# Holding the left keys and values of a memory-augmented recurrence by slot, with fewer and wider left matmuls

## The chip, the cores and the metric

The kernel runs on one core of one Trainium2 chip. The metric is the device time of one execution in microseconds; lower is better. Before the change the median of three runs is 1785.58 us (1778.69 to 1788.85).

## What is computed

The result is the sum of the input, an attention with memory, and a dense GELU block, all on 2048 tokens of width 1024 in bf16. The dense block reads all tokens at once. The attention is a recurrence: 64 segments of 32 tokens one after the other, where each segment sees 8 memory rows, and the first 8 rows of its own output are the memory of the next one.

```python
mem = mem0                                  # [8, 1024]
for s in range(64):
    xs = xn[:, 32 * s:32 * s + 32, :]
    h = concatenate([mem, xs], axis=1)      # 40 rows
    q, k, v = h @ Wq, h @ Wk, h @ Wv        # 32 heads of 128
    scores = where(mask, q @ k.T * scale, -1e9)   # memory rows see by the causal order of 40
    o = softmax(scores) @ v @ Wo
    mem = o[:, :8, :]
    outs.append(o[:, 8:, :])
out = x + concatenate(outs) + (gelu(xn @ w1 + b1) @ w2 + b2)
```

## The kernel before, in words

**Two stages.** The first (until about 410 us) makes the layer norm and the dense block, and turns the normalized rows into per-segment tiles in DRAM. The second is the recurrence; the change is in it alone, but for a few loads at the border.

**Weights.** A segment needs Wq, Wk, Wv and Wo whole, 64 tiles of 512 KB ("units", written as a letter, a block of rows and a half of the heads). 47 of them stay in SBUF. 17 a segment are streamed through a ring of six buffers (`RING`, `start_stream`, L273 to L285): when PE is done with one streamed unit, its buffer goes to the next in the order of use. Two of the 17 don't come from DRAM: they are kept in PSUM banks, and VectorE copies them into the buffer (`copy_bits`, L273), each as two halves of 128x512 uint32. The strings of `PLACED`, one for each of the four places of a segment in its group (`i4 = s % 4`), say at which unit of each pass of eight a streamed unit stands.

**Passes.** A segment goes through K, Q, K, Q, V, V (two halves of 16 heads; eight units each, `half_pass`, matmuls at L830) and then 16 output units (L1089). A unit of a pass is four matmuls that use four column groups of the array at once, with 512 columns each. PE's order is the order in which the code is written; the functions handed to a pass in `at` are issued after the unit with that number. `scores` (L947, L953), `sums` (L985, L991) and `values` (L1039, L1045) of one half of the heads are put between units of later passes in that way.

**Main and left rows.** The stationary operand of a projection holds 32 rows. For a segment these "main" rows are 24 of its tokens and the 8 memory rows. The remaining 8 tokens of each segment are "left" rows: those of four segments are put together in a second stationary tile (`hrL`), and one "left pass" of eight units makes their keys, queries or values for four segments. Each group of four segments has six left passes. In the old kernel they stand at i4 = 3 (K of half 0, V of half 1), 0 (K of half 1, V of half 0), 1 and 2 (Q). So a part of the left rows belongs to the next group while the present one isn't finished: `keep_q` saves queries in PSUM, and `moved_values` (L1191) holds the left values of half 1 in a tile of their own until they may be written. The first six resident units of the next left pass are issued at the end of the segment before ("lead", `lead_products`), where PE would wait for the memory rows.

**Attention of left rows.** In `scores`, each of 16 heads has one matmul of its main keys with 40 query columns (L947) and one of its left keys (32 rows of four segments) with 16 columns (L953). Four heads run at once in the four column groups. As left keys of all four segments are met, a mask by segment (`mask_left`, L977) takes out three quarters of the left probabilities. In `values`, four column blocks c each have a pair of matmuls of 64 rows with the main values (L1039, 80 columns) and a pair with the left values (L1045, 32 columns).

**Around it.** The key rows come out of PSUM by ScalarE (L882), and VectorE transposes them in blocks of 32 (L896); queries take L909 and L913 in two halves (`turn_q`). `q_left` (L925) puts the left queries of this segment into the first eight columns. `put_mem` (L320, L330) turns the 8 memory rows into the next segment's tile; L1243 adds the dense block's part to the result, which is loaded from DRAM (`hr_home<-res_d`). At i4 = 1, and in the last segment, the output pass also makes the 32 left rows, with four column tiles of 512 columns instead of two (`left_o`). Loads other than weights are issued by ScalarE in the first seven segments and by GpSimd after that; weights go through SP's queue.

## Time and profile before

| | |
|---|---|
| median of three runs | 1785.58 us |
| the profiled execution | 1788.29 us |
| its span, first to last instruction | 1786.6 us |
| granted TensorE clock | 0.998 |
| ScalarE work | 670.5 us |
| GpSimd work | 300.4 us |
| HBM read and written | 573.43 MB and 28.90 MB |

The profile is one execution. Each row of a group has a line of the kernel, an engine, an operation with what it writes and reads, the number of instructions, then the busy time with the mean of one in ns, and the idle time of the engine ahead of it with what ended that. Rows of the timeline have the start in us from the span's start, the time that a piece took, and the instructions merged in it. PE's durations hold some 0.17 us of latency for each matmul; matmuls overlap, so that intervals between starts tell what one costs. "issue" stands for idle time that nothing in the profile explains.

### The profile page before, as it was taken

Reading aid. Unit: us, or ns where it says so; the run is one execution under the profiler, and the core shown is the slowest. Engines: PE = TensorE matmul, PEld = TensorE weight load, DVE = VectorE, ACT = ScalarE, POOL = GpSimd, SP = SyncE. Lnnn points to the kernel's source line nnn. Section 1 sums busy time; section 2 is a strip of 40 time slices with the busy share of each in tenths; the row PEclk is TensorE's granted clock in tenths of the full one; section 3 lists DMA queues with packets and bytes.
Section 4 is the critical chain, followed back from the end, with each engine's and each line's share of the span. In section 5 each row is a group of like instructions: output and inputs, shape, how many; then the busy total and the mean of one; then the engine's idle time right before and its main releaser. Section 6 shows DMA issues by size and latency. Waiting matters only on the chain.

```text
span 1786.6 us, 70503 instructions
## 1 busy us (share of the span) xinstructions
PE 1697.1 (95%) x30600; PEld 867.5 (49%) x30600; DVE 987.9 (55%) x2642; ACT 670.5 (38%) x1709; POOL 300.4 (17%) x586
## 2 busy tenths in 40 slices
PE   9999999998999999999999999999999999999988
PEld 5444444444445544444545444454445445445444
DVE  7657483825555555555555555555555555555544
ACT  6334251603333333333333333343334333333333
POOL 0000002401231111111121211111121111111111
PEclk9999999999999999999999999999999999999999
DMA  9455312779999999999999999999999999999998
GB/s 278 146 167 169 91 45 71 267 277 335 387 390 388 387 374 383 380 383 367 393 378 382 374 381 393 389 388 389 375 387 400 389 389 394 380 378 396 378 376 316
DMA packets 232827, 594.37 MB, mean 333 GB/s; under 512 B 57715, under 2 KB 88035, under 8 KB 232516
## 3 DMA queue, kind: packets, MB, share of 16 engines
q1 hardware_dynamic: 197584, 567.08, 84.3%
q0 software_dynamic: 16896, 16.85, 2.8%
q10 hardware_dynamic: 18036, 5.94, 1.3%
q8 instruction: 239, 3.92, 0.9%
q14 instruction: 72, 0.59, 0.1%
HBM read 573.43 MB, written 28.90 MB: 337 GB/s over the span
## 4 chain that ended last, share of the span: by engine, by line
PE 70%; DMA 18%; DVE 4%; issue 3%; ACT 3%; ACTq 1%; SPq 1%; DVEq 0%
PE acc L830 36%; PE acc L1089 11%; PE ps L534 10%; DMA u<-Wc_O 10%; PE ps L662 6%; DMA u<-Wc_V 5%; PE ps L693 3%; PE acc L1039 1%; ACTq L459 1%; ACT mixed L999 1%; PE mixed L947 1%; SPq L521 1%; DMA hr_home<-res_d 1%; DVE pd_main L1012 1%; PE mixed L320 1%
## 5 line engine op out<-in xcount | busy, mean ns | idle before, releaser
L830 PE MATMUL acc<-u,hr_home 128*32 128x512 bf16 x11520 | 763.6, 380 | 19.7 <-DMA u<-Wc_V 10.2
L830 PEld LDWEIGHTS <-hr_home 128*32 128x32 bf16 x12288 | 337.8, 96 | 303.2 <-issue 45.2
L830 PE MATMUL acc<-u,hrL 128*32 128x512 bf16 x2880 | 253.0, 382 | 4.0 <-DMA hrL<-rowsL_d 2.1
L534 PE MATMUL ps<-u 128*128 128x512 bf16 (+1 forms) x992 | 195.1, 358 | 0.4 <-DMA u<-in_B_w_dram 0.4
L273 DVE TENSOR_SCALAR u<-kept 128x512 uint32<-128x512 uint32 x254 | 163.1, 684 | 48.0 <-PE acc L830 40.6
L1089 PE MATMUL acc<-u,d_oL 128*32 128x512 bf16 x2592 | 170.4, 380 | 13.0 <-issue 10.2
L882 ACT CAST d_oL<-acc 128x512 bf16<-128x512 f32 x143 | 82.0, 584 | 253.9 <-PE acc L830 220.9
L662 PE MATMUL ps<-u 128*128 128x512 bf16 x672 | 146.0, 379 | 0.0
L534 PEld LDWEIGHTS <-u 128*128 128x128 bf16 x992 | 91.6, 98 | 102.1 <-DMA u<-in_B_w_dram 0.6
L1089 PE MATMUL acc<-u,kq 128*32 128x512 bf16 (+1 forms) x2696 | 132.4, 320 | 8.1 <-DMA u<-Wc_O 6.4
L1012 DVE TENSOR_TENSOR pd_main<-kq,mixed 128x320 bf16<-128x320 bf16 x128 | 62.5, 488 | 129.2 <-ACT mixed L999 129.2
L909 ACT CAST kq<-acc 128x256 bf16<-128x256 f32 x256 | 89.4, 375 | 109.7 <-PE acc L830 76.6
L1089 PEld LDWEIGHTS <-kq 128*32 128x32 bf16 x3344 | 87.4, 96 | 84.0 <-ACT kq L1058 24.2
L1276 POOL DMA_DIRECT2D out_dram<-hr_home x168 | 85.4, 516 | 220.5 <-DVE hr_home L1243 220.5
L913 DVE STREAM_TRANSPOSE kq<-kq 128x256 bf16<-128x256 bf16 x256 | 98.2, 422 | 42.8 <-ACT kq L909 42.7
L886 ACT CAST kq<-acc 128x512 bf16<-128x512 f32 x128 | 75.2, 588 | 114.1 <-PE mixed L953 111.7
L977 DVE TENSOR_TENSOR kq<-kq,mixed 128x96 bf16<-128x96 bf16 (+1 forms) x256 | 38.1, 190 | 143.8 <-ACT kq L967 87.2
L830 PEld LDWEIGHTS <-hrL 128*32 128x32 bf16 x3072 | 86.3, 96 | 58.4 <-issue 3.7
L662 PEld LDWEIGHTS <-u 128*128 128x128 bf16 x672 | 65.5, 98 | 78.8 <-DVE u L619 0.4
L611 ACT ACTIVATE u<-ps,b1col 128x512 bf16<-128x512 f32 x112 | 76.5, 684 | 64.5 <-PE ps L534 61.7
L1089 PEld LDWEIGHTS <-d_oL 128*32 128x32 bf16 x2592 | 64.0, 96 | 69.5 <-issue 23.5
L999 ACT ACTIVATE mixed<-mixed,small_consts 128x160 f32<-128x160 f32 x256 | 94.2, 368 | 8.4
(127 smaller groups left out, 1910.5 us busy)
## 6 DMA issues: line engine op xcount, KB each, us to landing
u<-Wc_K SPq DMA_DIRECT2D x256, 512.0 KB
u<-Wc_V SPq DMA_DIRECT2D x256, 512.0 KB
u<-Wc_O SPq DMA_DIRECT2D x256, 512.0 KB
u<-Wc_Q SPq DMA_DIRECT2D x192, 512.0 KB
u<-in_B_w_dram SPq DMA_DIRECT2D x28, 512.0 KB
u<-in_A_Wq_dram SPq DMA_DIRECT2D x13, 512.0 KB
u<-in_A_Wv_dram SPq DMA_DIRECT2D x12, 512.0 KB
u<-in_A_Wk_dram SPq DMA_DIRECT2D x9, 512.0 KB
```

Of the source, the lines that this page charges most:

```text
L273: nc.vector.tensor_single_scalar(out=out, in_=in_, scalar=0, op=ALU.bitwise_or)
L534: nc.tensor.matmul(ps[:, SEG * s0:SEG * s1].rearrange("p (s t) -> p s t", t=SEG), lhsT=w1_sb[fb // 2][:, kt, (fb % 2) * P:(fb % 2 + 1) * P ...
L611: nc.scalar.activation(out=xb[:, :], in_=ps[:, :], func=ACT.Identity, bias=b1col[:, fb:fb + 1], scale=1.0)
L662: nc.tensor.matmul(ps[:, :], lhsT=gts[fc // 4][:, fc % 4, t * P:(t + 1) * P], rhs=w2_sb[fc // 2][:, fc % 2, cs], start=(fc == 0), stop=(fc ...
L830: nc.tensor.matmul(o, lhsT=lhs[:, i, :], rhs=m, start=(i == seq[0]), stop=(i == seq[-1]), tile_position=(0, 32 * j),)
L882: cp(out=out, in_=ps.rearrange("p (h e) -> p h e", e=32))
L909: nc.scalar.copy(out=q_home[:, h0:h1, NL:40], in_=ps[:, 32 * h0:32 * h1].rearrange("p (h e) -> p h e", e=32))
L913: nc.vector.transpose(out=half, in_=half)
L999: nc.scalar.activation(out=mixed[:, 160 * b:160 * b + 160], in_=mixed[:, 0:160], func=ACT.Exp, scale=-1.0, bias=off[:, b:b + 1],)
L1012: nc.vector.tensor_tensor(out=pdA.rearrange("p c b q -> p b c q"), in0=prA[:, None, :, :].to_broadcast([P, 2, 4, 40]), in1=dd, op=ALU.mult,)
L1089: nc.tensor.matmul(acc[r0:r0 + rows, 0:256 * len(blocks)], lhsT=lhsT, skip_group_check=True, rhs=o_columns(t, k, blocks), start=start, sto ...
L1276: loads.dma_start(out=out_flat[rows, 256 * j:256 * j + 256], in_=res[32 * j:32 * j + NX, :])
```

## The change

Left rows of a group are put in the order (token, segment) instead of (segment, token), so that the column `[..., i4]` of every fourth element is the 8 rows of one segment ("slot"). With that:

- `scores` takes the left keys of only this segment: 8 rows of four heads make one stationary tile of 32 columns, and one matmul meets it with the 16 left query columns of all four heads, 64 columns. The mask takes out the products of unlike heads.
- left values are laid out by slot too (`by_slot`, two transposes on VectorE), so that `values` has one pair of left matmuls with 128 columns for all four blocks.
- the left rows are renewed slot by slot (`renew_left`, copies on GpSimd, on VectorE in the first seven segments) in one tile that both groups share. Left passes stand at i4 = 0 (K, K), 1 (V of half 0), 2 (Q of half 0, V of half 1), 3 (Q of half 1); the double output pass stands at i4 = 3. Queries and values are made in the last group as well.
- the left accumulators are taken out of PSUM as soon as their last product is issued (`left_done`), ahead of the main ones of the same pass; `turn_qL` copies on ScalarE.
- `keep_q`, `moved_values` and the special cases of the last segment go. The strings of `PLACED` and some places change.

The core of the diff:

```diff
-SCORES_0 = (6, 6, 6, 5)
+SCORES_0 = (6, 6, 6, 6)
-ATTEND = (0, 0, 0, 1)
-VALUES_0 = ((4, 4), (4, 4), (4, 4), (3, 5))
-SUMS_1 = (6, 7, 6, 5)
+ATTEND = (0, 0, 1, 0)
+VALUES_0 = ((4, 4), (4, 4), (3, 5), (4, 4))
+SUMS_1 = (6, 6, 5, 7)
...
-    "..SS...." ".S..S..." "S....S.." "....S..S" "....S..." "S..S...S" "...S..S." "S....S.S",
-    "...SS..." ".S..S..." "..S..S.." "....SS.." ".S......" "S..S...S" "...S..S." "S....S.S",
-    ".SS....." "S...S..." "S....S.." "....S..S" "....S..." "S..S...S" "...S..S." "S....S.S",
-    "..SS...." ".S..S..." "S.....S." "....S..S" "....S..." "...SS..S" "...S..S." "S....S.S",
+    "..SS...." ".S..S..." "S....S.." "S......S" "S......." "S.S.S..." "...S.S.." "S....S.S",
+    ".SS....." "S...S..." ".S.S...." "....S..S" "....S..." "S..S.S.." "...S..S." "S....SS.",
+    "..SS...." ".S..S..." "S.....S." "....S..S" "..S....." "...SS..S" "...S..S." "S....SS.",
+    "...SS..." ".S..S..." "..S..S.." "....SS.." ".S......" "S..S...S" "...S..S." "S....SS.",
...
+    def renew_left(rows, s0, s1, eng):
+
+        eng.tensor_copy(
+            out=hL.rearrange("p k (t s) -> p k t s", s=GRP)[:, :, :, s0:s1],
+            in_=rows.rearrange("p (k s t) -> p k t s", k=KT, s=GRP)[:, :, :, s0:s1],
+        )
...
-            left_k = [first or (i4 == 3 and more), i4 == 0]
-            left_q = [first or (i4 == 1 and more), first or (i4 == 2 and more)]
-            left_v = [i4 == 0, first or (i4 == 3 and more)]
-            left_o = i4 == 1 or final
+            left_k = [i4 == 0] * 2
+            left_q = [first or i4 == 2, first or i4 == 3]
+            left_v = [first or i4 == 1, first or i4 == 2]
+            left_o = i4 == 3
...
+                    if left and left_done and i == order[-1]:
+                        left_done(psL)
...
+            def by_slot(u, t):
+
+                nc.vector.transpose(out=t, in_=t)
+                nc.vector.transpose(
+                    out=VL[u].rearrange("p (s n) -> p s n", s=GRP), in_=t.rearrange("p (n s) -> p s n", s=GRP)
+                )
...
-                turn(ps, qL[u][:, :, :], nc.vector.tensor_copy)
+                turn(ps, qL[u][:, :, :], nc.vector.tensor_copy if first else nc.scalar.copy)
...
+                keys = ko_flat[u].rearrange("p (j n s) -> p j n s", j=4, s=GRP)
...
-                    for j in range(4):
-                        q = slice(32 * j, 32 * j + 32)
-                        nc.tensor.matmul(
-                            sB[q, c, :].rearrange("p (a b) -> p a b", b=NL), lhsT=kL[u][:, 4 * j + c, :],
-                            rhs=qL_ends[:, 4 * j + c, :, :],
...
+                for j in range(4):
+                    q = slice(32 * j, 32 * j + 32)
+                    nc.tensor.matmul(
+                        sB[q, :, :, :], lhsT=keys[:, j, :, i4], rhs=qL_ends[:, 4 * j:4 * j + 4, :, :],
...
+                place = qL_slots[0] if first or VALUES_0[i4][0] < VALUES_0[i4][1] else ko_slots[0]
+                pdB = q_all[:, 512:640] if u else place[:, :, i4]
...
-                    for r in rs:
-                        q = slice(64 * r, 64 * r + 64)
-                        nc.tensor.matmul(
-                            oV[r].rearrange("p c b (e q) -> p c b e q", q=NL)[:, c, :, ::4, :],
-                            lhsT=VL[u][q, c * P:(c + 1) * P], rhs=pdB[q, c, :, :, :],
...
+                for r in rs:
+                    q = slice(64 * r, 64 * r + 64)
+                    nc.tensor.matmul(
+                        av[r][:, 0:320].rearrange("p (n e q) -> p n e q", n=8, q=NL)[:, :, ::4, :],
+                        lhsT=VL[u][q, i4 * P:(i4 + 1) * P], rhs=pdB[q, :].rearrange("p (n a q) -> p n a q", n=8, q=NL),
...
-            psK, psKL = half_pass("K", 0, left_k[0], {})
+            psK, psKL = half_pass(
+                "K", 0, left_k[0], {0: [lambda: by_slot(i4 - 2, qL_flat[i4 - 2])]} if i4 >= 2 else {},
+                lambda ps: turn_kL(ps, 0),
+            )
...
+            def first_queries(ps):
+
+                turn_qL(ps, 0)
                 q_left(0)
+
+            psQ, psQL = half_pass("Q", 0, left_q[0], {} if left_q[0] else {1: [lambda: q_left(0)]}, first_queries)
             turn_q(psQ)
-            if left_q[0] and not first:
-                turn_qL(psQL, 0)
...
+            psQ1, psQ1L = half_pass("Q", 1, left_q[1], at, lambda ps: turn_qL(ps, 1))
+            if left_q[1]:
                 q_left(1)
             turn_q(psQ1)
-            if left_q[1] and not first:
-                turn_qL(psQ1L, 1)
```

More of the change, by code (lines that the diff above doesn't have):

```diff
@@ L511, in turn_R @@
                     pairs = [(res_d[seg + 1, :, :].rearrange("(j t) c -> t j c", j=4), rows)]
[L512 to L518 removed]
+                pairs += [(both[w][slot:SEG:GRP, :, :], halves[w][NX:SEG, :, :]) for w in range(2)]
                 for o, r in pairs:
@@ L797, in unit_done @@
                         small.popleft()()
-        hT, hL = nxt["hT"], nxt["hL"]
-        kL, VL = [None] * 2, [None] * 2
+        hT = nxt["hT"]
+        VL = [late.tile([P, 512], BF16, name=f"VL{u}") for u in range(2)]
         led = {}
@@ L870, in half_pass @@
                     if left and i not in ahead:
-                        product(w, i, t, hL, psL, order)
+                        product(w, i, t, hL, psL, order, True)
                     if first and (w, i, u) == IN_PSUM:
@@ L902, in turn_kL @@
             def turn_kL(ps, u):
-                kL[u] = left_keys[u]
-                turn(ps, kL[u], nc.vector.tensor_copy if first else nc.scalar.copy)
+                turn(ps, ko[u], nc.vector.tensor_copy if first else nc.scalar.copy)
             def turn_q(ps):
@@ L1175 @@
             st["V", 1] = values_out(psV1, v_home, nc.scalar.copy)
-            apart = left_v[1] and not first
-            if apart:
-                ahead_v = left_keys[1]
-                rows_out(psV1L, ahead_v, nc.scalar.copy)
+            if left_v[1]:
+                staged(1)(psV1L)
             if first:
-                left_values(1, psV1L)
+                by_slot(1, hr_home)
+                renew_left(left_rows_in, 0, 2, mover)
+                load_x_rows(s + 1, loads)
             loads.dma_start(out=homes[s % 2], in_=res_d[s + 1, :, :])
-            if first:
-                load_left_rows(g + 1, loads)
-            def moved_values():
-                VL[1] = late.tile([P, 512], BF16, name="VL1")
-                (nc.vector if s < EARLY_SEGS else nc.gpsimd).tensor_copy(out=VL[1].rearrange("p (h t) -> p h t", t=SEG), in_=ahead_v)
+            if i4 == 3 and g + 2 < NGRP:
+                load_left_rows(g + 2, left_rows_in[:, :], loads)
             at = {VALUES_1[i4]: [lambda: values(1, (0, 1))]}
-            if apart:
-                at[VALUES_1[i4] + 1] = [moved_values]
             psX = new_acc()
```

201 lines of the change are left out of this document (74 added, 127 removed).

## The prediction

> **What bounds the kernel now.** I read the page first, for the span and the busy shares.
>
> ```profile
> span 1786.6 us, 70503 instructions
> PE 1697.1 (95%) x30600; PEld 867.5 (49%) x30600; DVE 987.9 (55%) x2642; ACT 670.5 (38%) x1709; POOL 300.4 (17%) x586
> ...
> q8 instruction: 239, 3.92, 0.9%
> ```
>
> PE has work 95% of the time, and no other engine is near that. The diff touches only the recurrence, from about 430 us to the end, so next I asked for busy time by stretches of it: a long one, and the densest 5 us that I found. Columns are engine busy times with counts, granted clock, DMA share and GB/s.
>
> ```profile
> 1025.00:1030.00 5.00, 4.89 (x118) 2.34 (x104) 3.23 (x10) 3.02 (x8) 0.57 (x1) 1.00 1.03 416
> 700.00:1700.00 1000.00, 947.90 (x20968) 497.52 (x20962) 543.33 (x1490) 377.34 (x1069) 187.21 (x353) 1.00 1.01 385
> ```
>
> The weight stream is nearly as tight as PE: the DMA engines always have something to do, and 385 of the 416 GB/s that they can reach are used, 93%. So PE has some 7% that it could gain before the stream stops it. Who ends PE's idle time is in PE's waits (us in total, times, longest):
>
> ```profile
> PE mixed L953 <- issue: 11.2, 12, 2.0
> PE acc L1089 <- issue: 10.5, 15, 1.3
> PE acc L830 <- DMA u<-Wc_V: 10.2, 20, 1.1
> PE acc L1089 <- DMA u<-Wc_O: 8.7, 22, 0.8
> PE acc L830 <- issue: 6.0, 8, 1.3
> ...
> PE mixed L947 <- issue: 4.0, 7, 0.8
> ```
>
> The stream costs 18.9 us. The four "issue" rows cost 31.7 us in 42 waits, and nothing in the program explains them. One stands between two matmuls of the same weight tile:
>
> ```profile
> 1241.71 0.38 PE L830 MATMUL acc<-u,hr_home 128*32 128x512 bf16 x1
> 1243.10 1.04 PE L830 MATMUL acc<-u,hr_home 128*32 128x512 bf16 x15 [1.02 <-issue]
> ```
>
> I take them for late instruction blocks: the page's queue q8 has 239 packets for 61,200 PE and PEld instructions, so 256 instructions come in one packet, and in the long stretch (41,930 instructions in 1000 us) a packet is used up every 6.1 us. The stalls are longest where small matmuls use it up fastest (L953, L947). That is inferred, not shown.
>
> **The change, part by part.**
>
> *Left scores and left values.* One call of `scores` in which nothing waits, and one of `values`:
>
> ```profile
> 1214.74 0.19 PE L947 MATMUL mixed<-kq,d_oL 128*32 128x40 bf16 x4
> ...
> 1214.93 0.21 PE L953 MATMUL mixed<-kq,d_oL 128*32 128x16 bf16 x4
> 1214.97 1.49 PE L830 MATMUL acc<-u,hr_home 128*32 128x512 bf16 x24
> ```
>
> ```profile
> 1201.71 0.21 PE L1039 MATMUL acc<-pd_main,kq 64*128 64x80 bf16 x2
> ...
> 1201.94 0.18 PE L1045 MATMUL acc<-d_oL,VL 64*128 64x32 bf16 x2
> 1202.05 0.61 PE L830 MATMUL acc<-u,hr_home 128*32 128x512 bf16 x8
> ```
>
> 32 score matmuls take 0.23 us, 7.2 ns each; what counts is the interval, not the 0.2 us of latency. Sixteen left ones of 16 columns become four of 64. A group of four with 512 columns costs 0.2165 us (below), so one with 64 columns streams in 0.027 us, no more than four matmuls take at 7.2 ns: 12 x 7.2 = 0.086 us saved a call, 128 calls, 11.0 us. In `values` pairs follow at (1201.94 - 1201.71) / 7 = 0.033 us and the last one takes 0.11 us to the next pass. Eight pairs become five, the last with 96 more columns (0.04 us): 0.34 becomes 4 x 0.033 + 0.15 = 0.28 us, 0.06 saved. In 16 calls the halves run apart and save it twice: 8.4 us. Together **-19.4 us**; if the last pair hides its columns, -24.
>
> The new operands are read with a step of four elements (`keys[:, j, :, i4]`, `place[:, :, i4]`). No row shows such a matmul. At best it costs nothing. At worst I let it be four times slower, as if each element were fetched alone: 0.087 us for the weights of each of 128 calls, and 0.16 us for 64 calls of `values`, 21 us. I take nothing, since L830 already reads pieces of 32 elements at the speed of plain runs; the end stays in the range. The Trainium skill, "SBUF — State Buffer", Door 1, speaks of 16-byte lines that give full rate from two hits a line, so that up to eight bf16 may be stepped over; by it the price is nothing as well, and no row here can show it.
>
> *Instruction blocks.* Per segment 24 matmuls go in `scores` and 12 in `values`, each with its weight load: 72 instructions. A segment has about 886, by the long stretch's 41.93 a us and the time from one group's double output pass to the next one's in the chain of waits, 84.5 us for four segments:
>
> ```profile
> 1141.21 4.43 PE acc L1089 x80
> ...
> 1225.74 4.43 PE acc L1089 x80
> ```
>
> So 8% go. At an unchanged pace a block lasts 0.5 us longer, where a stall is 31.7 / 42 = 0.75 us on average. The bounds are 0 and -31.7; I take **-18**. The Trainium skill, "Runtime: NRT & Kernel Launch", Instruction fetch mechanics, calls the fetch at a block's border mostly hidden; by that this term would be nothing, the time 18 us more, and the issue rows speak against it.
>
> *Left passes.* They move to other segments, and after the change they also run in the last group: 96 passes become 100 (K 32, Q 34, V 34). The last segment's double output pass was in the old kernel a 17th; now there are 16.
>
> ```profile
> 1232.67 4.06 PE L830 MATMUL acc<-u,hr_home 128*32 128x512 bf16 x72
> ...
> 1236.78 1.49 PE L830 MATMUL acc<-u,hr_home 128*32 128x512 bf16 x24
> ```
>
> 18 groups less the drain are (4.06 - 0.38) / 17 = 0.2165 us each. Four passes of eight are +6.9 us, the output pass -3.5: **+3.4 us**. The sum of left work in a cycle of four segments is otherwise the same.
>
> *Waits that come in.* Here is what the change can lose. DVE is idle much of the time, but not at a segment's start. This is DVE in a segment whose kept weight tile is copied after the fifth key unit (as the new order has it in i4 = 3), with the key pass's first matmuls ahead of it; the score matmuls quoted at 1214.74 are the same segment's:
>
> ```profile
> 1209.35 0.82 PE L830 MATMUL acc<-low,hr_home 128*32 128x512 bf16 x12
> ```
>
> ```profile
> 1209.02 0.23 DVE L330 CAST hr_home<-mixed 128x64 bf16<-128x64 f32 x1 [0.31 <-PE mixed L320]
> 1209.34 0.29 DVE L1243 TENSOR_TENSOR hr_home<-kq,hr_home 128x256 bf16<-128x256 bf16 x1
> 1210.65 1.29 DVE L273 TENSOR_SCALAR u<-kept 128x512 uint32<-128x512 uint32 x2 [1.02 <-PE acc L830]
> 1211.96 0.71 DVE L896 STREAM_TRANSPOSE d_oL<-d_oL 128x512 bf16<-128x512 bf16 x1
> ...
> 1213.86 0.77 DVE L913 STREAM_TRANSPOSE kq<-kq 128x256 bf16<-128x256 bf16 x2 [0.91 <-ACT kq L909]
> ```
>
> (a) In i4 = 2 and 3 `by_slot` puts two transposes of 0.71 us behind L1243, ahead of the kept copy (L273). The second needs the first, so DVE is free at 1209.63 + 1.42 = 1211.05 and not at 1210.65. PE began the key pass at 1209.35 and uses the copied tile 12 units later, at 1211.95 without left units between; the copy would now end at 1212.34: 0.4 us of wait in i4 = 3. In i4 = 2 a left unit stands between, and it is 0.2.
> (b) In i4 = 2 the left queries (ACT copy, DVE transpose, `q_left`) now come ahead of `turn_q`; they came behind it.
>
> ```profile
> L882 ACT CAST d_oL<-acc 128x512 bf16<-128x512 f32 x143 | 82.0, 584 | 253.9 <-PE acc L830 220.9
> ```
>
> The scores at 1214.74 stand seven key units behind the query pass, which so ended at 1213.22; the last left product is three units older, 1212.57, and has drained at 1212.74. ACT's copy takes 0.58 us (to 1213.33), the transpose 0.71 (1214.04), `q_left` 0.2 (1214.25), and L913's pair 0.77: 1215.0, where it ended at 1214.63. `scores(0)` would wait 0.35 us.
> (c) In i4 = 3 the same happens ahead of `scores(1)`, where the old kernel already is late: the matmuls at 1241.23 stop for 0.29 us until L913 is done.
>
> ```profile
> 1239.80 0.49 DVE L1012 TENSOR_TENSOR pd_main<-kq,mixed 128x320 bf16<-128x320 bf16 x1 [1.17 <-ACT mixed L999]
> 1240.21 0.35 DVE L1024 TENSOR_TENSOR kq<-kq,mixed 128x64 bf16<-128x64 bf16 x2
> ...
> 1240.70 0.76 DVE L913 STREAM_TRANSPOSE kq<-kq 128x256 bf16<-128x256 bf16 x2
> ```
>
> ```profile
> 1241.23 0.48 PE L947 MATMUL mixed<-kq,d_oL 128*32 128x40 bf16 x4
> 1241.52 0.20 PE L953 MATMUL mixed<-kq 128*32 128x16 bf16 x4
> ```
>
> ACT is free of the sums at 1239.77 (when L1012 is released), its copy ends at 1240.35, the transpose, behind L1012 and L1024, at 1241.27, `q_left` at 1241.45, and L913's second half 0.77 later, at about 1242.1 instead of 1241.46: 0.6 us.
> Per group 0.2 + 0.4 + 0.35 + 0.6 = 1.55 us, in 15.5 groups **+24 us**. A residual load that lands late (L1243) adds to (a); where PE waits for something else anyway, nothing is added. Bounds 8 and 45.
>
> *What costs nothing.* `keep_q`, the second left product of `sums` and `moved_values` were off the path (DVE 55%, POOL 17% busy); the slot copies of `renew_left` go on POOL and have two or three passes of 1.7 us until the next left pass; ACT gets two copies of 0.58 us a group and is 38% busy. If that cover fails they show as waits before L830. The weights' bytes are the same, and so are the left rows' and results'. The smallest distance from freeing a slot to its tile's use, counted in units from the two order strings, is about 5.1 us in both. In the first segment the next rows are loaded later, but the wait for the left rows is gone; I call it even, within 3 us.
>
> *Sum.* -19.4 - 18 + 3.4 + 24 = -10. New PE waits let the stream catch up; of its 18.9 us I take 3 as covered: **-13 us**. The profiled execution took 1788.3 us (span 1786.6 and 1.7 around it), so 1775.3. The median of the three runs is 2.7 below it, and 1785.6 - 13 = **1772.6 us**.
>
> **The rivals.**
>
> 1. *The new waits decide* (slower). Place: DVE at the start of i4 = 2 and 3, and the turn of the queries. For it: L913 ends within 0.1 us of the scores already, and in (c) behind them. Against it: the matmuls that go leave slack only elsewhere. If they cost 45 us, and the blocks gain only 8, it is -19.4 - 8 + 3.4 + 45 = +21: 1807. It decides from (19.4 + 18 - 3.4 + 3) / 15.5 = 2.4 us a group.
> 2. *The stream is the bound* (no change). If 385 GB/s is all that the mix of small and large transfers gives, PE's time turns into waits for `u`: 1786. Against it: 416 GB/s in the dense stretch, and only 18.9 us of waits.
> 3. *The block stalls stay* (about no change): they hang on the place of the border, not on the count. Without the 18 us, 1790.6. The Trainium skill's page on the runtime, named above, would have it so.
> 4. *Steps of four are slow*: +21, 1794, less what it covers.
> 5. *All stalls go and the waits are few*: -24 - 28 + 3.4 + 8 = -41: 1745.
> 6. *The matmuls aren't saved*, if the four heads' wide ones were issued beside the old ones; the diff removes the loops, so I give it no chance.
>
> **How the numbers follow.** About 0.5%, 8.9 us, is what a measurement of this kernel can tell from no change. Chances: my forecast 0.44 (its own range 1758 to 1784, so a third of it lies within 0.5%), rival 1 0.23, rival 2 0.12, rival 3 0.06, rival 4 0.05, rival 5 0.10. Faster: 0.44 x 0.68 + 0.10 + 0.02 = 0.42; slower: 0.23 + 0.04 + 0.03 = 0.30 (half of rivals 3 and 4); the rest, 0.28, within. The range 1750 to 1804 leaves out about half of rival 5 and some two fifths of rival 1, 0.15 in all.
>
> **What would show it.** Right: `scores` in 0.15 us where it doesn't wait, `values` in 0.28; about 28,400 matmuls (30,600 - 64 x 36 + 128 - 48); the issue rows of PE's waits at 10 to 18 us; DVE's L273 copy in i4 = 3 ending some 0.4 us later against the segment's start, and PE waiting for it; score matmuls that stop for DVE in i4 = 2 and 3. Wrong: waits for `u` that grow by as much as the matmuls shrink (rival 2), an interval over 0.03 us after a group of left score matmuls (rival 4), issue rows unchanged (rival 3), or waits behind DVE over 2.4 us a group (rival 1).

## The result, and the profile after

The changed kernel takes **1797.71 us** (median of 7 runs, 1796.02 to 1802.71), the kernel before 1779.55 us in the same comparison (7 runs, 1776.52 to 1788.85). The ratio is 1.0094, 95% interval [1.0069, 1.0119]: **slower by 0.9%**. The time lies in the predicted range; the direction was predicted wrong. The profiled execution took 1802.7 us, with a granted clock of 0.995.

In what follows PE is TensorE (PEld its weight loads), DVE is VectorE, ACT ScalarE and POOL GpSimd. First the page of the changed kernel, and its long stretch from 700 to 1700 us (busy times with counts, granted clock, DMA share, GB/s):

```profile
span 1801.0 us, 65865 instructions
PE 1702.4 (95%) x28354; PEld 844.9 (47%) x28374; DVE 1017.2 (56%) x2592; ACT 694.0 (39%) x1743; POOL 300.3 (17%) x603
...
q8 instruction: 222, 3.64, 0.8%
```

```profile
700.00:1700.00 1000.00, 940.36 (x19046) 476.25 (x19049) 555.78 (x1431) 389.64 (x1080) 188.59 (x371) 0.99 0.99 380
```

2246 matmul records and 4638 instructions are gone, about as many as the diff says (the prediction counted 2224 matmuls), and yet PE is no less busy, and idle for 1801.0 - 1702.4 = 98.6 us, where it was 1786.6 - 1697.1 = 89.5. So the question is which waits came. PE's waits after the change (us in all, times, longest):

```profile
PE acc L832 <- DVE hr_home L1209: 18.9, 11, 4.1
PE acc L1069 <- DMA u<-Wc_O: 18.4, 36, 1.1
PE acc L832 <- DMA u<-Wc_V: 15.7, 34, 1.3
...
PE acc L832 <- DMA u<-Wc_K: 2.9, 6, 1.1
...
PE acc L832 <- DMA u<-Wc_Q: 2.6, 8, 0.7
PE mixed L945 <- DVE kq L920: 2.1, 7, 0.5
PE acc L832 <- issue: 1.4, 2, 1.2
...
PE acc L832 <- DVE u L275: 0.9, 3, 0.4
```

Three things are to be seen. The issue rows, 31.7 us before, are nearly gone (1.4 us, and a row of 0.3). The waits for weights (`u`) have doubled, from 18.9 to 18.4 + 15.7 + 2.9 + 2.6 = 39.6 us. And the longest row is new, with single waits of up to 4.1 us: PE waits for L1209, the add of the residual (the dense block's part of a result), which was L1243. The wait stands behind the first key pass of the next segment, at its first query matmul, whose accumulator takes the place in PSUM that L1209 reads. Here is the longest one:

```profile
1027.82 3.60 PE L832 MATMUL acc<-u,hr_home 128*32 128x512 bf16 x32 [4.09 <-DVE hr_home L1209]
```

What L1209 waits for is in DVE's waits, and who was late with that in GpSimd's:

```profile
DVE pd_main L1209 <- DMA pd_main<-resL_d: 40.7, 14, 5.7
```

```profile
POOL pd_main L1177 <- DMA hr_home<-res_d: 41.3, 9, 5.0
```

L1177 issues the load of the left residual (the dense block's part of the group's 32 left rows, 64 KB) in the output pass of i4 = 3. Before the change the same instruction waited for PE, and DVE hardly waited for its load:

```profile
POOL pd_main L1208 <- PE acc L1045: 40.3, 14, 3.6
```

```profile
DVE pd_main L1243 <- DMA pd_main<-resL_d: 3.5, 6, 1.0
```

The load depends on PE alone: its buffer is free when the last value matmuls have read it. After the change it waits for the *landing of another load*, of which it needs nothing. GpSimd's timeline in one group, and DVE's at the end of the segment (start, us, instruction, idle time before it with what ended it):

```profile
1190.21 0.56 POOL L1161 DMA_DIRECT2D hr_home<-res_d  x1 [4.63 <-PE mixed L984]
1190.85 0.55 POOL L298 DMA_DIRECT2D left_rows_in<-rowsL_d  x1
1195.80 0.56 POOL L1177 DMA_DIRECT2D pd_main<-resL_d  x1 [4.40 <-DVE u L275]
```

```profile
1200.65 0.42 DVE L1209 TENSOR_TENSOR pd_main<-acc,pd_main 128x256 bf16<-128x256 f32 x1 [1.07 <-DMA pd_main<-resL_d]
1200.99 0.42 DVE L1209 TENSOR_TENSOR hr_home<-acc,hr_home 128x256 bf16<-128x256 f32 x1
```

The last value matmuls ended at 1193.8 here, but the load went at 1195.80 and L1209 began over a microsecond late. The row puts the wait down to L275, whose end came last by the profile; the residual that was issued at 1190.21 had landed at 1195.49, 0.31 us before the load went. Over all groups the pattern is strict. In the 13 in which the load of the left rows (L298) stands between the residual (L1161) and the left residual (L1177) on GpSimd's queue, L1177 is issued 0.31 us after the residual has landed, 2.0 to 4.5 us after the last value matmul (the row of 41.3 us counts nine of them; the profile puts the other four down to PE and DVE). In the two last groups there is no L298, and it goes about 0.4 us after that matmul, as in all 15 groups before the change.

The new matmuls can be read from two rows of the timeline each (`scores` where nothing waits; then `values` of the first half and of the second):

```profile
1206.59 0.27 PE L945 MATMUL mixed<-kq,d_oL 128*32 128x40 bf16 x16
1206.70 0.21 PE L951 MATMUL mixed<-kq,d_oL 128*32 128x64 bf16 x4
1206.73 0.39 PE L832 MATMUL acc<-u,hr_home 128*32 128x512 bf16 x4
...
1213.28 0.32 PE L1019 MATMUL acc<-pd_main,kq 64*128 64x80 bf16 x8
1213.43 0.28 PE L1025 MATMUL acc<-d_oL,VL 64*128 64x128 bf16 x2
1213.64 0.61 PE L832 MATMUL acc<-u,hr_home 128*32 128x512 bf16 x8
```

```profile
1193.46 0.32 PE L1019 MATMUL acc<-pd_main,kq 64*128 64x80 bf16 x8
1193.61 0.22 PE L1025 MATMUL acc<-kq,VL 64*128 64x128 bf16 x2
1193.76 0.83 PE L1069 MATMUL acc<-u,d_oL 128*32 128x512 bf16 x12
```

`scores` went from 0.23 to 1206.73 - 1206.59 = 0.14 us. `values` went from 0.34 to 0.30 us in the second half of the heads, and *up* to 0.36 us in the first.

### The profile page after: what moved, and what is told of

Same layout as the page of the kernel before. It is cut to its first block, busy times and chain, and to the rows that moved or that the text cites. A ratio compares the mean times of both kernels' runs of the same rounds, so it can differ in the third digit from the quotient of the medians.

```text
span 1801.0 us, 65865 instructions
## 1 busy us (share of the span) xinstructions
PE 1702.4 (95%) x28354; PEld 844.9 (47%) x28374; DVE 1017.2 (56%) x2592; ACT 694.0 (39%) x1743; POOL 300.3 (17%) x603
## 4 chain that ended last, share of the span: by engine, by line
PE 37%; DMA 24%; DVE 7%; issue 4%; ACT 3%; POOL 0%; DVEq 0%; ACTq 0%; SPq 0%; POOLq 0%
PE acc L832 26%; DMA u<-Wc_O 11%; PE acc L1069 7%; DMA u<-Wc_V 4%; DMA pd_main<-resL_d 3%; DMA u<-Wc_Q 3%; DMA u<-Wc_K 3%; DVE kq L920 1%; PE acc L1019 1%; DVE u L275 1%; ACT mixed L992 1%; DMA hr_home<-res_d 1%; DVE qL L904 1%; PE mixed L945 1%; DVE pd_main L1000 1%
## 5 line engine op out<-in xcount | busy, mean ns | idle before, releaser
L832 PE MATMUL acc<-u,hr_home 128*32 128x512 bf16 x11520 | 766.6, 382 | 44.8 <-DVE hr_home L1209 18.9
L832 PE MATMUL acc<-u,hrL 128*32 128x512 bf16 x3008 | 259.6, 381 | 1.4 <-issue 1.4
L1069 PE MATMUL acc<-u,d_oL 128*32 128x512 bf16 x2560 | 165.4, 381 | 7.1 <-DMA u<-Wc_O 7.0
L275 DVE TENSOR_SCALAR u<-kept 128x512 uint32<-128x512 uint32 x254 | 162.0, 679 | 10.8 <-PE acc L832 7.4
L1069 PE MATMUL acc<-u,kq 128*32 128x256 bf16 (+1 forms) x2688 | 132.2, 319 | 13.9 <-DMA u<-Wc_O 11.4
L1236 POOL DMA_DIRECT2D out_dram<-hr_home x168 | 85.4, 516 | 251.9 <-DVE hr_home L1209 251.4
L969 DVE TENSOR_TENSOR kq<-kq,mixed 128x96 bf16<-128x96 bf16 x128 | 26.2, 205 | 167.2 <-ACT kq L962 86.5
```

The costliest lines, as they stand in the source:

```text
L275: nc.vector.tensor_single_scalar(out=out, in_=in_, scalar=0, op=ALU.bitwise_or)
L832: nc.tensor.matmul(o, lhsT=lhs[:, i, :], rhs=m, start=(i == seq[0]), stop=(i == seq[-1]), tile_position=(0, 32 * j),)
L1069: nc.tensor.matmul(acc[r0:r0 + rows, 0:256 * len(blocks)], lhsT=lhsT, skip_group_check=True, rhs=o_columns(t, k, blocks), start=start, sto ...
L1236: loads.dma_start(out=out_flat[rows, 256 * j:256 * j + 256], in_=res[32 * j:32 * j + NX, :])
```

## The experiments

**Theory.** GpSimd has room for two loads of 128 rows in flight. The change puts a third between them, so the left residual is issued late, DVE's add is late, PE loses some 2 us a group, and the stream has no reserve from which to make this up. **Rival.** The stream is the bound in any case: what the matmuls and the blocks give comes out as waits for `u`, and the late residual only takes their place.

### Moving the third load, or putting it on another queue

The left rows of the group after next are not needed for two segments. In the first kernel they are asked for behind the left residual:

```diff
             loads.dma_start(out=homes[s % 2], in_=res_d[s + 1, :, :])
-            if i4 == 3 and g + 2 < NGRP:
-                load_left_rows(g + 2, left_rows_in[:, :], loads)
...
                     loads.dma_start(
                         out=st["resL"], in_=resL_d[g, :, :]
                     )
+                    if g + 2 < NGRP:
+                        load_left_rows(g + 2, left_rows_in[:, :], loads)
```

> The changed kernel with one load moved: the left rows of the group after next are asked for behind the left residual (in the output pass) and no longer between the residual and the left residual on GpSimd's queue. Queue theory (GpSimd's queue has room for two such loads, the third waits until the first has landed): the left residual's load is issued 0.4 us after the last left value matmul in all groups, where the changed kernel has 2.0 to 4.5 us in 13 of 15; the waits of the residual add L1209 for it fall from 40.7 us to under 8, PE's 18.9 us behind L1209 go, and with the stream catching up in the same place the time falls by 19 to 40 us, to 1758 to 1779. Stream theory (the weight stream is the bound and gives out later whatever the residual does): the left residual lands early as well, but PE's waits for u grow from 36.9 us by what L1209 no longer costs, and the time stays within 6 us of the changed kernel, 1792 to 1804.

In the second they stay at their place, on ScalarE's queue:

```diff
-                load_left_rows(g + 2, left_rows_in[:, :], loads)
+                load_left_rows(g + 2, left_rows_in[:, :], nc.scalar)
```

> The changed kernel with the same load left at its place and put on ScalarE's queue. Queue theory: what counts is the number of loads ahead on GpSimd's own queue, so the left residual again is issued 0.4 us after the last left value matmul, and the time is that of the kernel with the moved load within 6 us (1758 to 1779). Traffic theory (three loads of 64 KB close together are too much for the DMA engines, on any queue): the left residual still lands 4 us or more after the last left value matmul, L1209 still waits over 25 us in all, and the time stays at 1792 to 1804.

Measured: 1771.68 us (1766.6 to 1777.7; ratio to the kernel before 0.9949 [0.9925, 0.9972]) and 1771.16 us (1765.07 to 1775.23; 0.9936 [0.9907, 0.9964]). Against 1797.71 us that is 26 us for the place of one load of 64 KB, 13 times. In both the left residual is issued 0.4 us after the last value matmul in nearly all groups (0.7 us in one), and L1209 waits for it 2.6 and 4.0 us in all. In the first kernel the same queue shows where the wait went. It is now the left rows that wait for the residual's landing, and nobody waits for them:

```profile
POOL left_rows_in L298 <- DMA hr_home<-res_d: 35.2, 13, 3.4
POOL pd_main L1175 <- PE acc L1025: 30.3, 13, 2.4
```

PE's longest waits in the first kernel:

```profile
PE acc L832 <- DMA u<-Wc_V: 20.1, 38, 2.2
PE acc L1069 <- DMA u<-Wc_O: 14.5, 29, 1.7
PE mixed L945 <- DVE kq L920: 4.0, 14, 0.5
...
PE acc L832 <- DMA u<-Wc_Q: 2.4, 6, 0.6
PE acc L832 <- DMA u<-Wc_K: 1.5, 4, 0.5
```

The row behind L1209 is gone, and the waits for `u`, 38.5 us in all, have not grown (39.6). So the rival is out as the cause of the loss. On ScalarE's queue the same bytes at the same time do no harm, so it isn't traffic either.

### Is it room, and is it rows that fill it?

The kernel gives GpSimd's DMAs 320 bytes a partition for their descriptors (`SCRATCH`). The next kernel leaves the order of the changed one alone and gives them 448:

```diff
-SCRATCH = 320
-SMALL = 3776
+SCRATCH = 448
+SMALL = 3648
...
```

> The changed kernel, with its loads in their old order, and with 448 bytes a partition in place of 320 for the descriptors of GpSimd's DMAs (two tiles change places to make room). Room theory: 320 bytes hold two 64 KB loads of 128 rows and not three, 448 hold three; the left residual is issued 0.4 us after the last left value matmul in every group, PE's waits behind L1209 go, and the time is that of the kernel with the moved load, 1766 to 1778. If GpSimd holds the third load back for another reason (the number of loads, an order of its own), nothing changes: 1792 to 1804.

The other one is the kernel *before*, with a third load that carries 2 KB in place of 64, but has 128 rows as well:

```diff
             loads.dma_start(out=homes[s % 2], in_=res_d[s + 1, :, :])
+            if left_o and loads is nc.gpsimd:
+                loads.dma_start(out=small_consts[:, 8:16], in_=rowsL_d[g, :, 0:8])
```

> The kernel before with one more load on GpSimd's queue, between the residual and the left residual of i4 = 1: 16 bytes from each of 128 rows (2 KB in all, into columns that nothing reads), in the 13 or so groups in which GpSimd issues these loads. Room theory: what fills the room is rows and not bytes, so the left residual's load waits for the residual's landing as in the changed kernel; DVE's waits at L1243 for it rise from 3.5 us to over 25 us, and the time rises by 10 to 26 us, to 1790 to 1806. Traffic theory: 2 KB are nothing, the time stays at 1777 to 1784.

With 448 bytes: 1770.69 us (1766.49 to 1776.28; 0.9938 [0.9916, 0.996]). In the old order of the loads, the left residual again waits for PE and not for a landing:

```profile
1165.39 0.57 POOL L1162 DMA_DIRECT2D hr_home<-res_d  x1 [4.48 <-PE mixed L985]
1166.00 0.55 POOL L299 DMA_DIRECT2D left_rows_in<-rowsL_d  x1
1168.35 0.55 POOL L1178 DMA_DIRECT2D pd_main<-resL_d  x1 [1.80 <-PE acc L1026]
```

The kernel before with the 2 KB load: 1793.78 us (1785.52 to 1813.13; ratio 1.0058 [1.0038, 1.0079]), so 10 us slower than without it, by the ratio. (The profiled execution is the longest of the ten, with a span of 1810.5 us and a granted clock of 0.993; only which waits appear is read from it.) The wait of the changed kernel is there, and in all 15 groups the left residual goes 0.31 us after the residual has landed:

```profile
POOL pd_main L1210 <- DMA hr_home<-res_d: 47.1, 11, 5.1
```

```profile
DVE pd_main L1245 <- DMA pd_main<-resL_d: 29.6, 16, 4.7
PE acc L830 <- DVE hr_home L1245: 11.4, 10, 3.5
```

The effect can thus be taken out of the changed kernel by 128 bytes, and put into the old one by 2 KB of traffic. It hangs on rows in flight, not on bytes. Nor is it the number of transfers: with 320 bytes, the changed kernel's GpSimd issues four stores of 24 rows (L1236) within 1.8 us in each of 42 segments, and the first lands 2.7 us or more after the fourth was issued.

The Trainium skill, "DMA: Bandwidth & Descriptors", Terms and The descriptor swizzle, gives 16 bytes for a descriptor, and nine descriptors on each of the 16 DMA engines for the write side of a GpSimd transfer of 1 MiB to 128 partitions. If a load of 64 KB or 2 KB to 128 rows has nine as well, and each 16 bytes a partition make room for one descriptor on each engine, both of which are assumed here, an estimate from that page is 20 for 320 bytes, room for 18 and not for 27, and 28 for 448, room for 27. The runs agree with that.

### What the matmuls and blocks are worth without the rest

The kernel before, with its own order, leaves out as many left matmuls after its first segment as the change saves:

```diff
-                    for j in range(4):
+                    for j in range(4) if c == 0 or first else ():
                         q = slice(32 * j, 32 * j + 32)
                         nc.tensor.matmul(
                             sB[q, c, :].rearrange("p (a b) -> p a b", b=NL), lhsT=kL[u][:, 4 * j + c, :],
...
-                    for r in rs:
+                    for r in rs if c == 3 or first else ():
                         q = slice(64 * r, 64 * r + 64)
                         nc.tensor.matmul(
                             oV[r].rearrange("p c b (e q) -> p c b e q", q=NL)[:, c, :, ::4, :],
```

> The kernel before, with its own order and queues, which after its first segment leaves out 12 of the 16 left score matmuls and 6 of the 8 left value matmuls of each call, so that it issues as many as the changed kernel does there (its left outputs lack what these add). It prices the first two terms of the prediction alone. By the prediction: matmuls -19 and block stalls -18, 1781 becomes 1742 to 1750. By the kernel with the moved load, in which the block stalls went from 31.7 to under 3 us and the waits for u rose by 20 us: the issue rows of PE go to under 6 us, the waits for u rise from 18.9 to some 35 us, and the time is 1750 to 1764. If the stream alone is the bound: 1770 to 1781.

Measured: 1754.89 us (1753.27 to 1759.42; 0.9849 [0.9822, 0.9876]), 27 us less. Its issue rows are down to 1.3 us and a few of 0.3, with 222 packets on q8, and the waits for `u` are up from 18.9 to 55.1 us, where some 35 were expected:

```profile
PE acc L1089 <- DMA u<-Wc_O: 41.2, 78, 1.7
PE acc L830 <- DMA u<-Wc_V: 11.9, 30, 1.2
...
PE acc L830 <- DMA u<-Wc_Q: 2.0, 4, 0.7
```

PE's idle time is what it was, 1754.5 - 1664.4 = 90.1 us for 89.5, and its busy time is 32.7 us less. So the prediction's first two terms are real (27 us are left of the 37 foreseen), but the stream's share was far too small: about as much idle time as the blocks gave back (30 us) went to the stream (36 us), and what was left to gain is PE's busy time.

### Is it the stream's rate?

The kernel with the moved load fetches half of each streamed query, key and value tile and uses that half twice:

```diff
-            nc.sync.dma_start(out=t[:, :], in_=copies[unit])
+            if n >= 4 * STREAMED and unit[0] != "O":
+                nc.sync.dma_start(out=t[:, 0:1024], in_=copies[unit][:, 0:1024])
+                short.add(n)
+            else:
+                nc.sync.dma_start(out=t[:, :], in_=copies[unit])
...
```

> The kernel with the moved load, which from the fifth segment on loads only the first half of each streamed query, key and value tile and uses it twice (its outputs are not the reference's; the matmuls are as many and as long). That takes about 37% of the stream's bytes away. If PE's waits for u (38.5 us) are the stream's rate, as the pairs with and without the left queries and with fewer matmuls suggest, they fall under 8 us and the time falls by 28 to 38 us, to 1734 to 1744. If they come from when slots become free, and not from bytes, they stay above 25 us and the time above 1760.

Measured: 1733.58 us (1731.17 to 1736.2; 0.9718 [0.9672, 0.9763]), 38 us less than the kernel with the moved load. The long stretch of this kernel (259 GB/s), of the kernel with the moved load (391) and of the kernel before without the left matmuls (393):

```profile
700.00:1700.00 1000.00, 967.24 (x20056) 488.58 (x20052) 580.68 (x1503) 410.13 (x1134) 197.40 (x387) 1.00 0.80 259
```

```profile
700.00:1700.00 1000.00, 958.63 (x19596) 486.59 (x19586) 569.71 (x1467) 402.47 (x1115) 193.37 (x382) 1.00 1.01 391
```

```profile
700.00:1700.00 1000.00, 943.30 (x19702) 480.19 (x19698) 554.33 (x1523) 386.37 (x1095) 190.31 (x359) 1.00 1.02 393
```

Under 8 us of waits for `u` were expected and 16.2 are left, but the time is what was expected, and a little better: a third less stream is worth about 38 us even with the load moved. The rows of waits give only part of that: the waits for `u` fell by 22 us, and PE's busy time fell by another 22 us (1696.9 to 1674.7) although it has the same matmuls, while other waits grew a little. The starts of the matmuls tell where the busy time went. From one matmul of the projections or the output to the next, the intervals of up to 0.3 us add up to 1002.7 us with the moved load (20,758 of them, 48.3 ns in the mean) and 1011.9 us with the short stream (20,837, 48.6 ns); the longer ones add up to 97.4 us (170) and 50.2 us (91). So matmuls run no slower beside the denser stream. There are more stops, and the first part of each lies under the 0.38 us that the profile gives the matmul ahead of it, and counts as busy.

No kernel of the study got past 393 GB/s over the long stretch. The 416 of a dense 5 us, from which the prediction took 7% of reserve, is not a rate that this kernel holds.

### The waits for the turned left queries

Without the copy and the transpose of the left queries after the first segment, in the changed kernel and in the one with the moved load:

```diff
             def turn_qL(ps, u):
+                if not first:
+                    let_go(ps)
+                    return
                 turn(ps, qL[u][:, :, :], nc.vector.tensor_copy if first else nc.scalar.copy)
```

> The changed kernel without the copy and the transpose of the left queries after the first segment (the left queries of the first group are used throughout). It takes away what delays scores(0) in i4 = 2 and scores(1) in i4 = 3. By the prediction's terms (b) and (c) it gains 0.35 + 0.6 us a group, 15 us, 1783. Queue theory: those waits are 0.3 to 0.4 us a group and what they give is partly taken back by the late left residual, so 0 to -8 us, 1790 to 1798.

> The kernel with the moved load, without the copy and the transpose of the left queries after the first segment (the first group's left queries are used throughout). It takes away the stops of the score matmuls in i4 = 2 (0.39 us a group) and i4 = 3 (0.7 us a group), 17 us in 15.5 groups. If PE's own time is the bound: 1772 becomes 1753 to 1757. If the stream takes back what PE gains: waits for u rise above 38 us by most of it, and the time is 1762 to 1771.

Measured: 1794.57 us (1790.66 to 1800.22; ratio to before 1.0076 [1.0048, 1.0103], beside 1.0094 for the changed kernel, so the difference of 3 us is not sure; the queue theory had 0 to 8), and 1765.49 us (1763.89 to 1768.88; 0.9907 [0.988, 0.9933]), 6 us less than with the moved load alone. The stops are as the prediction has them. Here is `scores(1)` of i4 = 3 in the changed kernel, with its 16 main matmuls drawn out by DVE's transposes; the call takes 1187.53 - 1187.08 = 0.45 us where 0.14 would do, and there is a gap of some 0.26 us ahead of it in the mean:

```profile
1187.08 0.60 PE L945 MATMUL mixed<-kq,d_oL 128*32 128x40 bf16 x16
...
1187.53 1.05 PE L832 MATMUL acc<-u,hr_home 128*32 128x512 bf16 x16
```

Of 0.37 and 0.70 us of such stops a group with the moved load, 0.01 and 0.20 are left without the left queries; that is some 13 us in all, for 6 us of time. The waits for `u` of the last kernel are 20.7 + 18.1 + 3.3 + 1.7 = 43.8 us, 5 more. More than half was given back, part of it to the stream.

### The step of four in the values

In the changed kernel the left value matmul reads every fourth column of its moving tile in the first half of the heads (`place[:, :, i4]`), and columns in a row in the second (`kq`); mean duration of one in ns behind the comma:

```profile
L1025 PE MATMUL acc<-kq,VL 64*128 64x128 bf16 x128 | 14.7, 219 | 1.2 <-DVE VL L897 1.2
...
L1025 PE MATMUL acc<-d_oL,VL 64*128 64x128 bf16 x94 | 13.1, 276 | 0.0
L1025 PE MATMUL acc<-qL,VL 64*128 64x128 bf16 x34 | 9.4, 275 | 0.0
```

The kernel with the moved load gets a tile of its own for them:

```diff
+    pdB_0 = hrp.tile([P, 128], BF16, name="pdB_0")
...
-                pdB = q_all[:, 512:640] if u else place[:, :, i4]
+                pdB = q_all[:, 512:640] if u else pdB_0[:, :]
```

> The kernel with the moved load, and with the normalized left scores of the first half in a tile of their own, 128 columns in a row instead of every fourth of 512. In the changed kernel the left value matmul takes 275 ns with the step of four (first half) and 219 ns without it (second half). Step theory: the first half's falls to 219 ns as well, the call from 0.36 to 0.30 us, at most 64 x 0.057 = 3.6 us in all, of which the stream takes a part: 1768 to 1772. If the 56 ns belong to something else in the first half (another source tile, another bank), they stay.

```profile
L1025 PE MATMUL acc<-pdB,VL 64*128 64x128 bf16 x128 | 17.8, 218 | 0.0
```

The 57 ns go, so they belong to the step. Time: 1767.76 us (1761.98 to 1774.77; 0.9913 [0.9882, 0.9943]), 4 us less than with the moved load, about the bound of what was expected and within the spread.

### The scores one unit later

```diff
-SCORES_0 = (6, 6, 6, 6)
+SCORES_0 = (6, 6, 7, 6)
...
-ATTEND = (0, 0, 1, 0)
+ATTEND = (1, 0, 1, 1)
...
```

> The kernel with the moved load and plain values, and with the scores issued one unit later where their matmuls stop for the turned queries: scores(0) of i4 = 2 behind the eighth key unit, scores(1) of i4 = 3 and 0 behind the second value unit. The stops are 0.4, 0.7 and 0.65 us a group; one unit is 0.38 us, so up to 17 us of them go. By the run without the left queries, in which 17 us of stops gave 6 us of time, 1762 to 1767. If the later scores make the sums or the values late instead, their waits for DVE and ACT (L1000, L1019) grow and the time is 1770 or more.

Measured: **1763.93 us** (1759.73 to 1770.21), ratio to the kernel before 0.9895 [0.986, 0.9929]. This version is faster than both kernels: 1.0% below the one before, and 34 us below the changed one. How much of the last 4 us is the places and how much spread can't be told.

### Sixteen narrow left score matmuls again

To test what the issue stalls hang on, the kernel with the moved load issues the same left scores in pieces of 16 columns:

```diff
-                    nc.tensor.matmul(
-                        sB[q, :, :, :], lhsT=keys[:, j, :, i4], rhs=qL_ends[:, 4 * j:4 * j + 4, :, :],
-                        start=False, stop=True, skip_group_check=True, tile_position=(0, 32 * j),
-                    )
+                    for c in range(4):
+                        nc.tensor.matmul(
+                            sB[q, c, :, :], lhsT=keys[:, j, :, i4], rhs=qL_ends[:, 4 * j + c, :, :],
+                            start=False, stop=True, skip_group_check=True, tile_position=(0, 32 * j),
+                        )
```

> The kernel with the moved load, in which the wide left score matmul of each block of rows is cut into four of 16 columns again, so that 16 left score matmuls are issued a call as in the kernel before, with the same results. It adds 1536 matmuls and as many weight loads to PE's instructions, two thirds of what the change took away. Pace theory of the issue stalls (blocks of 256 instructions used up faster than they come): PE's issue rows, about 1 us in the kernel with the moved load and 31.7 in the kernel before, rise to 10 us or more, the call takes 0.09 us longer (11 us in all), and after the stream has taken its part back the time is 1778 to 1790. If the stalls hang on something else that the change took away: issue rows under 4 us, and the time 1771 to 1778.

Measured: 1787.08 us (1776.76 to 1797.51; 1.002 [0.9994, 1.0045]), 15 us more than with the moved load (13 by the two ratios). That is what the wide matmul is worth together with the stops that it avoids; for the two the prediction had 11.0 us and some two thirds of 18. The issue rows are three:

```profile
PE acc L832 <- issue: 3.6, 5, 1.1
PE mixed L952 <- issue: 1.7, 2, 1.0
...
PE acc L1020 <- issue: 0.7, 2, 0.5
```

6.0 us, where the kernel with the moved load has 0.5: between the two expectations. With 234 packets on q8 (222 without these matmuls, 239 before) the stalls come back, but by a fifth and not by two thirds. They don't follow the count alone.

What they are can be read from the traces. PE and its weight loads run 61,380 instructions in the kernel before (their waits counted), 239.8 times 256, and q8 has 239 packets of 16 KB. Counted through in runs of 256, all 42 stops of the kernel before stand at one place, number 193 or 194 of the run (173 or 174 in the changed kernel), and each ends 1.2 to 1.6 us after a packet has landed. So they are the late instruction blocks that the prediction inferred. From a packet's landing to the crossing of that place it is 1.7 us in the median of the recurrence before the change (under 1.65 us at 103 of 218 crossings), 2.4 us with the narrow matmuls (44 of 212), 2.8 us with the moved load (15 of 201), and 4.0 us with the short stream, which has no issue row at all. The reserve thus shrinks with PE's pace and with a denser stream, and stops appear where it is used up, which fits that they don't go in proportion to the instructions.

## Why the prediction was wrong, point by point

| step | predicted, us | measured |
|---|---|---|
| left scores | -11.0 | 0.23 to 0.14 us a call, 128 calls: -11.5 |
| left values | -8.4 | 0.34 to 0.36 and 0.30 us a call: about -1 |
| block stalls | -18 | issue rows 31.7 to 1.7: -30 |
| left passes, output pass | +3.4 | counts as predicted (3200 left matmuls, 100 passes); not measured alone |
| new waits for DVE and ACT | +24 | stops of `scores` 0.76 to 1.75 us a group: about +15 |
| stream | -3 | waits for `u` 18.9 to 39.6: +21 |
| loads ("what costs nothing") | 0 | late left residual: +26 |

The column adds up to about +23, and the medians differ by 18.2. Rows of waits and differences of times are mixed in it, and the terms are not independent, so it isn't a sum that has to come out.

**The step that failed is the paragraph on what costs nothing.** It counted the bytes of the left rows' loads and found them equal. It did not ask what was queued behind such a load where the change put it: on GpSimd's queue between the residual and the left residual. Under (a) the prediction did name a residual that lands late, but gave it no price. Moving that one load, and nothing else, gives 1771.68 us, 0.9949 of the kernel before, where 1772.6 had been forecast: the direction of the forecast was lost in this step. That the level comes so near is partly chance, since the other terms were off as well and made up for each other:

- *Left values* were reckoned at plain speed. The step of four elements in the moving operand about halves the rate (57 ns on 128 columns, about what these take at a plain rate, by the 216.5 ns for 512). As weights, in `scores`, the same step makes a load longer (107 ns against 94 for the plain ones of L945), but a call of 20 matmuls takes 0.14 us all the same, so that nothing of it is seen in the time. So the bound of "four times slower" held, and the value chosen inside it was wrong for one of the two uses. The Trainium skill, "SBUF — State Buffer", Door 1, lets up to eight bf16 be stepped over at full rate; the trace agrees nearly for the weights (107 ns against 94) and not for the moving operand (275 ns against 219), and the measurement decides.
- *Block stalls* were understood rightly and sized too small: they went almost wholly, in the changed kernel and in the old one without the left matmuls, out of proportion to the 8% of instructions that went. The Trainium skill, "Runtime: NRT & Kernel Launch", Instruction fetch mechanics, calls the fetch at a block's border mostly hidden; that fits the rows after the change (1.7 us), not those before (31.7 us), whose stops all stand at one place in 256 instructions.
- *New waits.* (a) failed: PE waits 0.9 us in all for the kept copy. (b) and (c) held: 0.40 and 0.57 us a group, for 0.35 and 0.6. But `scores(1)` of i4 = 0 stops as well (0.65 us, 0.16 before), and old stops went, of `scores(1)` at i4 = 2 (0.31 us) and of `scores(0)` at i4 = 3 (0.15 us); the sum left both out. All calls together stop for 1.75 us a group after the change and 0.76 before, 1.0 us more or some 15 us in 15.5 groups. (These are means over the timeline's calls from the fifth segment on, from the matmul ahead of a call to the one behind it, less what an undisturbed call takes and less the issue waits.)
- *Stream.* It was given 3 us of relief from new PE waits. It took more than 20 us instead: each microsecond that PE gains brings the ring closer to empty, and 393 GB/s is the most that any kernel here kept up.

Rival 1 had the sign, with its price at DVE's transposes; those were not the place. Rival 2's mechanism is at work in all these kernels, but it takes back gains and doesn't turn them into a loss: with the load moved the change is faster.

## What to carry to other kernels

A moved DMA is judged by the queue that it is moved into, not by its bytes: list what stands behind it and when that is due, and look at GpSimd's rows for an issue that waits for the landing of a load of which it needs nothing. Where the weight stream runs at 380 to 390 GB/s of a best of 393, count only a part of what PE gains, and take the stream's reserve from the best sustained rate, not from its densest 5 us. In a strided layout, price the step for each operand by itself: it was hidden for weights and halved the rate of the moving operand.

## What the runs showed of the hardware

- With 320 bytes a partition for its descriptors GpSimd had two loads of 128 rows in flight and no third, whether that carried 64 KB or 2 KB; with 448 bytes it had three. The third was issued 0.31 us after the first had landed. Four stores of 24 rows were in flight together at 320 bytes.
- A moving operand of 128 bf16 columns with a step of four took 275 ns, a plain one 219 ns. A load of 32 stepped columns of weights took 107 ns, a plain one 94 ns, which was hidden.
- A third less stream (391 to 259 GB/s) took 38 us off, of which the rows of PE's waits show 22; the same matmuls were 22 us less "busy", though none ran faster (48.3 and 48.6 ns between starts).
- PE stopped for late instruction blocks 42 times (31.7 us) when the blocks landed 1.7 us ahead of their crossing in the median, 9 times at 2.4 us, twice at 2.8 us, and never at 4.0 us.
